# Four order edits in one fused training kernel: last forward norms, a scale and a memset, a gradient row, and the even inverse sums

## The chip, the cores and the metric

The kernel runs on one core of one Trainium2 chip. The metric is the device time of one execution in microseconds; lower is better. Before the change three runs took 1480.12, 1479.07 and 1468.7 us, so the median is 1479.07 us.

Five engines work side by side, each through its own queue in order: TensorE (PE, matmuls; its weight loads are PEld), VectorE (DVE), ScalarE (ACT), GpSimd (POOL) and SyncE (SP, which here only issues DMAs). An instruction that waits holds everything behind it in its queue.

## The reference

The kernel computes the output of one block and its nine gradients (a forward and a backward pass). Cut to what matters:

```python
def A(x, w_r, w_i):                 # spectral filter
    X = rfft2(x.astype(float32)) * (w_r + 1j * w_i)
    return irfft2(X).astype(bfloat16)
def B(x, w1, b1, w2, b2):           # channel MLP on a second layernorm
    h = gelu(layernorm(x) @ w1 + b1)
    return h @ w2 + b2
sa, ca, ga, sb, cb, gb = (silu(c) @ w_mod).reshape(6, D)
h = layernorm(x) * (1 + ca) + sa;  x = x + ga * A(h)
h = layernorm(x) * (1 + cb) + sb;  x = x + gb * B(h)
# returned: x and the gradients of x, w_r, w_i, w1, b1, w2, b2, c, w_mod
```

There are S = 2048 tokens, D = 1024 features and F = 3584 hidden features; everything is bfloat16.

## The kernel before

The order of the instructions in each queue is made when the program is built: a planner goes through the instructions with estimated times and gives each engine, whenever it is free, the ready instruction that stands first in the program (those in `tc.high_priority()` go first of all). `tc.issue_after(x)` adds, for the instructions in its block that run on x's engine, an edge of order only: they are planned behind x. `tc.add_manual_dep` does the same for one pair. Buffers of the same `tag` share one place in memory: a new tile waits until every user of the old one is done, stores included.

The tokens are four chunks of 512 (index i or b). The stages, in the order of the program:

- **Start.** Rows of `silu(c) @ w_mod` (`mod_block`), cosine and sine matrices made by POOL, DVE and ACT (`gen_mats`; `em1` holds them twice, as made and scaled), and `gBoT`, the output gradient transposed and scaled.
- **`ph_part`** (line 743): the product of `B_w2` with `gBoT`, 28 pieces. It depends on no forward work, so it fills PE between the steps of the forward spectral core.
- **First layernorm and folds.** For each chunk `ln_dve` or `ln_mix`, `norm_act`, then additions that fold tokens and features into even and odd halves (`fold_tok`, `fold_d`, `fold_pair`) into `fbuf`. `css` (tag `px0`) is cleared by a memset before the core.
- **Forward spectral core** (`spectral_core(True, ...)`): `s_fwd` for the four classes CE, SE, CO, SO (even and odd cosine and sine), eight `pair` steps, which multiply by the filter on DVE and write `R`; `s_inv` for the classes; then for each chunk `consume_fwd`. The four even-class rows of `R` are written by pairs 0 to 3, the odd ones by pairs 4 to 7.
- **`consume_fwd`** ends, for each chunk, with two layernorms: the second statistics pass is `ln_dve(tmp, 2, i)` (its square root is line 466, in `ln_fin`), then `norm_act(tmp, tmp, 2, i)` (line 500), then SP stores `tmp` to `d_n3`. `tmp` lies in `ct`, tag `fr`.
- **MLP forward**: a list written out by hand mixes `z_block` (n = 0 to 27; n = 7b + g) with steps of `bo_pass` (line 912). A `z_block` runs 32 matmuls `pz` into four PSUM banks, four ACT copies with bias into `zb` (line 864), then the gelu and its derivative on ACT (lines 866, 870, 872) and DVE (lines 867, 873 and `tt`, line 186). `hh`, the gelu, goes to one of eleven slots: `hhB` for n = 0, 1, `hhC` for 2, `hhA` for 3 to 10. `hhA` has tag `fr`. `zb` and its companions are one of two sets:

```python
n = b * 7 + g
zb, av, bv, sg, ph = gts[n % 2]
hh = hh_slots[n % 11]
```

- **MLP backward** (`pg_pass`, line 1009), with layernorm gradients, and the folds of the gradient into `fbuf2` (`fold_quarter`; the last one is `fold2_in[3]`).
- **Gradient of `w_mod`**: row r of six is made in eight steps of 128 rows. `gmod_ring` (lines 1045 to 1059) uses three buffers: SP loads a slice of `w_mod`, DVE multiplies and sums it (line 1056) and writes the product into the same buffer (line 1058), POOL stores it (line 1059). Row 5 runs before the backward core, rows 3 and 4 one step at a time beside it (`beside_bwd`), rows 2, 1, 0 after it.
- **Backward spectral core** (`spectral_core(False, ...)`). Between its steps `fill(k)` runs k products of the gradient of `w2` (line 1134; 16 matmuls each). Each pair of products needs a transposed load of `d_hh` (line 1290, `hhsA`, `hht` or part of `otl`), in a ring of three slots during the pairs; the two slots `hhsA` share tag `px1` with `au`. Four products follow each pair. `mid()` puts the last column sums between the even and the odd `s_fwd`. Before pair 6 stand the two even `s_inv`, after pair 7 the two odd ones.
- **End**: `consume_bwd` for each chunk, filled with products of the gradient of `w1` (line 1328), and the last rows of the gradient of `w_mod`.

Of the kernel before, what the change touches and what calls it, by code (L numbers as in the profile page):

```python
# [13 lines left out]
ACT = mybir.ActivationFunctionType  # L14
# [4 lines left out]
S = 2048  # L19
# [16 lines left out]
def kernel(  # L36
# [403 lines left out]
    def gen_mats():  # L440
        for cl, colv, modn in ((CE, kev, 2048), (SE, kev, 2048), (CO, kod, 4096), (SO, kod, 4096)):
            sm = (smA, smB)[cl % 2]
            rows, n = (rowo, 4) if cl % 2 else (rowe, 2)
            if cl == SE:
                nc.gpsimd.memset(kev[:, 0:1], 512.0)
            for r in range(0, n, 2):
                trig(sm[:, cl // 2, r:r + 2, :], colv, rows[r:r + 2], 2, 512, modn, cl < 2)
            nc.gpsimd.dma_start(out=d_SF[:, cl, 0:n], in_=sm[:, cl // 2])
        for cl, colv, modn in ((CE, jf[:, 0:256], 1024), (SE, jf[:, 1:257], 1024), (CO, jod, 2048), (SO, jod, 2048)):
            trig(em1[:, 0, 2 * cl:2 * cl + 2, :], colv, rowe, 2, 256, modn, cl < 2)  # L450
        nc.gpsimd.tensor_scalar(out=em1[:, 1], in0=em1[:, 0], scalar1=2.0 / (S * D), scalar2=None, op0=ALU.mult)
# [11 lines left out]
        ln_fin(sv[:, :, 2:3], sv[:, :, 1:2], sv[:, :, 3:4], 1.0 / D, row, i)  # L463

    def ln_fin(var, nmean, std, scale, row, i):
        nc.scalar.activation(out=std, in_=var, func=ACT.Sqrt, bias=eps_c[:], scale=scale)
# [28 lines left out]
        ln_fin(mv[:, :, 1:2], mv[:, :, 2:3], mv[:, :, 3:4], 1.0, row, i)  # L495

    def norm_act(out4, in4, row, i):
        for q in range(4):
            t = 4 * i + q
            nc.scalar.activation(out=out4[:, q, :], in_=in4[:, q, :], func=ACT.Identity,  # L500
                                 scale=stats[:, row, 0, t:t + 1], bias=stats[:, row, 1, t:t + 1])

    last_pu = [None]
    last_po = [None]
# [18 lines left out]
    def spectral_core(fwd, fb, sms, em, css, pt, evac_u, evac_c, evac_v, consume, o4tag, pfs=None, fill=lambda n: None, mid=lambda: None, beside=lambda n: None):  # L523
# [79 lines left out]
        def s_inv(cl, smi):  # L603
            Vt = reg.tile([P, 8, 512], BF16, name=f"V{cl}", tag=f"uv{cl}")
            Vs[cl] = Vt
            for c8 in range(8):
                dc, h = c8 // 2, c8 % 2
                k0 = (0, 1, 2, 1)[dc] + 256 * h
                base = k0 + (PW if (dc >= 2) == (cl < 2) else 0)
                pv = (ps_f if cl % 2 == 0 and c8 % 2 and not fwd else ps_s)("pv")  # L610
                for m in range(4):
                    k = (m // 2 + cl // 2) % 2
                    out, m0, m1 = (pv[:], 0, 3) if cl % 2 else (pv[:, k * 256:(k + 1) * 256], m // 2 * 2, m // 2 * 2 + 1)
                    nc.tensor.matmul(out, lhsT=R[:, cl * 4 + m, :, :].rearrange("p x w -> p (x w)")[:, base:base + 255:2],
                                     rhs=smi[:, cl // 2, m, :], start=(m == m0), stop=(m == m1))
                with tc.high_priority():
                    evac_v(Vt[:, c8, :], pv[:])
# [21 lines left out]
        pair_load(0)  # L639
        for par in range(2):  # L640
            for m in range(4):
                if par == 1 and m == 2:
                    s_inv(CE, smis[0])
                    s_inv(SE, smis[0])
                pair(par * 4 + m, par, m)
                if par * 4 + m < 7:
                    pair_load(par * 4 + m + 1)
                beside(par * 4 + m)
                if par == 0 and m == 0:
                    load_smi()  # L650
                if par == 0 and m > 0:
                    v = 0 if fwd else 1
                    if m == 1:
                        gm = reg.tile([P, 12, 256], BF16, name="gm", tag="gm")
                        for cl in (CO, SO):
                            with tc.issue_after(ld_in[0].ins):
                                nc.sync.dma_start(out=gm[:, 2 * cl:2 * cl + 2, :], in_=d_E[:, v, 2 * cl:2 * cl + 2, :])
                    else:
                        cl = (CE, SE)[m - 2]
                        for h in range(2):  # L660
                            with tc.issue_after(ld_in[0].ins):
                                nc.sync.dma_start_transpose(out=gm[:, 2 * cl:2 * cl + 2, h * P:(h + 1) * P],
                                                            in_=d_E[:, v, 2 * cl + h, :])
        s_inv(CO, smis[1])
        s_inv(SO, smis[1])
        with tc.issue_after(r_in[0].ins):
# [97 lines left out]
    for i in range(4):  # L764
        x4, fb = x4s[i], fbuf[:, i]
        if i == 0:
            with tc.issue_after(u_in.ins):
                ln_dve(x4, 0, i)
        elif i > 0:
            ln_mix(x4, 0, i, fb)  # L770
        else:
            ln_act(x4, 0, i, fb)
        norm_act(fb, x4, 0, i)
        tt(fb, fb, bcn(opca_row, 4), ALU.mult)
        fold_tok(fb, x4)
        if i % 2 == 0:
            fold_d(fb, fb, x4[:])
        else:
            pv_ = fbuf[:, i - 1]
            fold_pair(fb, pv_, fb, x4[:], x4s[i - 1][:, 0:2, :])  # L780
            tt(pv_[:, 0, :], pv_[:, 0, :], saf, ALU.add)
    css = reg.tile([P, 2, 2, 2 * PW], BF16, name="cs01", tag="px0")
    nc.gpsimd.memset(css[:], 0.0)

    def consume_fwd(i, o4, tmp, tmp2, x4, eb):
        unfold_d(o4, tmp)
# [60 lines left out]
    def z_block(b, g0, g1):  # L847
# [3 lines left out]
        for g in range(g0, g1):  # L851
# [4 lines left out]
            for k in range(4):  # L856
                fc = g * 4 + k
                pz = (ps_s, ps_d)[k % 2]("pz")
                for cch in range(NDC):
                    with ordered():  # L860
                        last_pe[0] = nc.tensor.matmul(pz[:], lhsT=w1s[g][:, cch, k * P:(k + 1) * P], rhs=n3T[:, cch, :],  # L861
                                                      start=(cch == 0), stop=(cch == NDC - 1))
                with tc.high_priority():
                    nc.scalar.activation(out=zb[:, k, :], in_=pz[:], func=ACT.Identity, bias=b1_col[:, fc:fc + 1], scale=1.0)  # L864
            with after_ev():
                nc.scalar.activation(out=av, in_=zb, func=ACT.Square)  # L866
            nc.vector.tensor_scalar(out=av, in0=av, scalar1=GC, scalar2=1.0, op0=ALU.mult, op1=ALU.add)
# [561 lines left out]
```

## Time and profile before

| | |
|---|---|
| median of three runs | 1479.07 us (1468.7 to 1480.12) |
| profiled execution, its own time | 1477.05 us |
| its span, first to last instruction | 1475.1 us |
| mean granted TensorE clock | 0.98 |
| PE busy | 1378.1 us, 93% |
| DVE busy | 1075.7 us, 73% |
| ACT busy | 749.3 us, 51% |
| POOL busy | 368.9 us, 25% |
| moved by DMA | 321.66 MB, mean 218 GB/s |

Times in the trace count from the start of the span. A row of the timeline gives the start, the duration, the engine, the line, the operation, output and input, the number of merged instructions and, in brackets, how long the engine stood idle before it and what ended that. A row of the windows gives for each engine the busy time in a stretch, then the granted clock and the share of time that the DMA engines were busy. Overlapping instructions of one engine are both counted in full, so a duration can hold a wait for a port or for a predecessor.

### The profile page before, as it was taken

To read this page: it belongs to the slowest core of one execution; us is meant where nothing else is said; L and a number is where in the kernel's file an instruction comes from. 1 tells how busy PE (TensorE), PEld (TensorE's weight loads), DVE (VectorE), ACT (ScalarE), POOL (GpSimd) and SP (SyncE) were. 2 spreads that over 40 slices of the span, in tenths; PEclk is the share of its full clock that TensorE was granted. 3 is DMA by queue.
4 is the path that set the end of the run, shared out by engine and by line. 5 is a ranking of instruction groups with operands and counts; after the bars stand their busy time and mean duration, and the time that the engine had idled before them with its cause. 6 is when DMAs were issued, how large, how long until landed. Compare 5 with 4: busy or idle time off the path is not lost. (4 is left out here: it accounts for less than half of the span.)

```text
span 1475.1 us, 18310 instructions
## 1 busy us (share of the span) xinstructions
PE 1378.1 (93%) x6705; PEld 651.9 (44%) x6835; DVE 1075.7 (73%) x1501; ACT 749.3 (51%) x1065; POOL 368.9 (25%) x446
## 2 busy tenths in 40 slices
PE   4979999899599999999999999999998989999997
PEld 2535555444244444444444444444554535444443
DVE  5995878797799787887520899887566677998633
ACT  4675555768787765666206563332522425443211
POOL 5620631201012122112111011010334431322423
PEclk9999999999899999999999999999999999999999
DMA  9962564799488867698998266287699998667994
GB/s 334 280 214 72 152 206 149 243 299 324 172 219 270 262 233 253 195 277 224 266 281 242 96 233 228 84 233 169 178 216 226 249 216 213 189 191 196 241 235 164
DMA packets 356063, 321.66 MB, mean 218 GB/s; under 512 B 207210, under 2 KB 298880, under 8 KB 355846
## 3 DMA queue, kind: packets, MB, share of 16 engines
q1 hardware_dynamic: 321990, 206.14, 52.8%
q0 software_dynamic: 33984, 114.36, 22.6%
q8 instruction: 53, 0.87, 0.3%
q14 instruction: 36, 0.29, 0.1%
HBM read 161.01 MB, written 110.15 MB: 184 GB/s over the span
## 5 line engine op out<-in xcount | busy, mean ns | idle before, releaser
L743 PE MATMUL pp<-gBoT,wt 128*128 128x512 bf16 x872 | 197.3, 382 | 7.1 <-DVE pho L749 5.8
L1009 PE MATMUL pg<-w1T,gzr 128*128 128x512 bf16 x877 | 196.9, 383 | 1.0
L1328 PE MATMUL gw1acc<-gzh,n3n 128*128 128x512 bf16 x876 | 193.8, 379 | 3.4 <-DMA gzh<-d_gz 2.4
L861 PEld LDWEIGHTS <-w 128*128 128x128 bf16 x896 | 87.5, 98 | 123.4 <-issue 20.0
L743 PEld LDWEIGHTS <-wt 128*128 128x128 bf16 x896 | 87.6, 98 | 110.5 <-issue 8.7
L1009 PEld LDWEIGHTS <-gzr 128*128 128x128 bf16 x896 | 87.3, 98 | 109.4 <-issue 7.2
L1328 PEld LDWEIGHTS <-n3n 128*128 128x128 bf16 x896 | 87.2, 98 | 107.8 <-issue 3.8
L861 PE MATMUL pz<-n3Ta,w 128*128 128x512 bf16 x440 | 99.5, 384 | 16.0 <-ACT gt L864 15.7
L1134 PE MATMUL gw2acc<-gB,hhsA 128*128 128x512 bf16 x438 | 99.4, 384 | 4.6 <-DMA hhsA<-d_hh 4.0
L861 PE MATMUL pz<-n3Tb,w 128*128 128x512 bf16 x437 | 98.4, 379 | 0.7 <-ACT gt L864 0.2
L912 PEld LDWEIGHTS <-hhA 128*128 128x128 bf16 x608 | 59.4, 98 | 75.0 <-issue 5.5
L864 ACT ACTIVATE gt<-pz,b_col 128x512 bf16<-128x512 f32 x112 | 72.7, 683 | 36.2 <-PE pz L861 35.7
L1141 ACT CAST gwo<-gw2acc 128x512 bf16<-128x512 f32 x46 | 26.7, 583 | 120.8 <-PE gw2acc L1134 75.8
L1332 ACT CAST gwo<-gw1acc 128x512 bf16<-128x512 f32 x50 | 29.1, 583 | 112.2 <-PE gw1acc L1328 92.1
L186 DVE TENSOR_TENSOR gt<-gt,gt 128x2048 bf16<-128x2048 bf16 x56 | 68.4, 1224 | 21.8 <-ACT gt L872 20.6
L186 DVE TENSOR_TENSOR ct<-ct 128x2048 bf16<-128x2048 bf16 x68 | 80.5, 1220 | 0.6
L870 ACT ACTIVATE gt<-gt 128x2048 bf16<-128x2048 bf16 x28 | 53.5, 1911 | 53.7 <-DVE gt L186 53.7
L1056 DVE CUSTOM_DVE_ANT_0 otl<-otl 128x1024 bf16<-128x1024 bf16 x24 | 29.1, 1224 | 55.9 <-DMA otl<-in_w_mod_dram 44.8
L1134 PEld LDWEIGHTS <-hhsA 128*128 128x128 bf16 x448 | 43.9, 99 | 57.7 <-DMA hhsA<-d_hh 5.1
L749 ACT CAST pho<-pp 128x512 bf16<-128x512 f32 x62 | 35.8, 582 | 45.9 <-PE pp L743 45.2
L866 ACT ACTIVATE gt<-gt 128x2048 bf16<-128x2048 bf16 x28 | 53.4, 1908 | 4.8 <-DVE w2sA L186 2.3
L872 ACT ACTIVATE gt<-gt 128x2048 bf16<-128x2048 bf16 x28 | 53.5, 1909 | 0.5
(335 smaller groups left out, 2535.3 us busy)
## 6 DMA issues: line engine op xcount, KB each, us to landing
gzr<-d_gz SPq DMA_DIRECT2D x28, 512.0 KB
wblk<-in_w_mod_dram SPq DMA_DIRECT2D x12, 1024.0 KB
out_dram<-otl POOLq DMA_DIRECT2D x48, 256.0 KB, 3.4
out_dram<-gwo POOLq DMA_DIRECT2D x96, 128.0 KB, 4.1
d_ph<-pho POOLq DMA_DIRECT2D x21, 512.0 KB, 4.4
d_hh<-hhA POOLq DMA_DIRECT2D x19, 512.0 KB, 5.0
w2sD<-in_B_w_dram SPq DMA_DIRECT2D x14, 512.0 KB
w2sA<-d_ph SPq DMA_DIRECT2D x14, 512.0 KB
```

The source lines that it names most:

```text
L186: return nc.vector.tensor_tensor(out=out, in0=a, in1=b, op=op)
L743: last_pe[0] = nc.tensor.matmul(pp[:], lhsT=wt[:, fg % 2, cch, k * P:(k + 1) * P], rhs=gBoT[j][:, cch, :], start=(cch == 0), stop=(cch == ...
L749: nc.any.tensor_copy(out=ov, in_=pv)
L861: last_pe[0] = nc.tensor.matmul(pz[:], lhsT=w1s[g][:, cch, k * P:(k + 1) * P], rhs=n3T[:, cch, :], start=(cch == 0), stop=(cch == NDC - 1))
L864: nc.scalar.activation(out=zb[:, k, :], in_=pz[:], func=ACT.Identity, bias=b1_col[:, fc:fc + 1], scale=1.0)
L866: nc.scalar.activation(out=av, in_=zb, func=ACT.Square)
L870: nc.scalar.activation(out=sg, in_=bv, func=ACT.Sigmoid, scale=2.0 * GK)
L872: nc.scalar.activation(out=bv, in_=bv, func=ACT.Sigmoid, scale=-2.0 * GK)
L912: last_pe[0] = nc.tensor.matmul(pbs[i][:], lhsT=hh[:, k, i * P:(i + 1) * P], rhs=wp[:, k, :], start=False, stop=(g == 6 and k == 3))
L1009: last_pg[0] = nc.tensor.matmul(pgs[i][:], lhsT=gzs[b, g][:, k, i * P:(i + 1) * P], rhs=w1Ts[g][:, k, h * KH:(h + 1) * KH], start=(g == 0 ...
L1134: nc.tensor.matmul(acc[:], lhsT=hh_of(fc)[:, t, :], rhs=gBs[t // 4][:, t % 4, h * KH:(h + 1) * KH], start=(t == 0), stop=(t == NT - 1))
L1328: nc.tensor.matmul(acc[:], lhsT=n3ns[t // 4][:, t % 4, cch * P:(cch + 1) * P], rhs=gz2[t // 8][:, t % 8, :], start=(t == 0), stop=(t == NT ...
```

## The change

Four edits, independent of each other:

1. In `gen_mats` the scaled copy of `em1` moves from POOL to ACT. The memset of `css` moves from POOL to DVE and is ordered behind the last addition of the forward fold.
2. The square root of the last chunk's last forward layernorm is ordered behind the fourth PSUM copy of `z_block` n = 3, and its four `norm_act` instructions behind the fourth PSUM copy of n = 4.
3. In the backward core the two even `s_inv` move from ahead of pair 6 to behind pair 7 and its fills. The forward core keeps them ahead of pair 6.
4. The DVE instructions of row 5 of the gradient of `w_mod` are ordered behind the last gradient fold.

```diff
-        nc.gpsimd.tensor_scalar(out=em1[:, 1], in0=em1[:, 0], scalar1=2.0 / (S * D), scalar2=None, op0=ALU.mult)
+        nc.scalar.mul(out=em1[:, 1], in_=em1[:, 0], mul=2.0 / (S * D))
...
-        nc.scalar.activation(out=std, in_=var, func=ACT.Sqrt, bias=eps_c[:], scale=scale)
+        sqrt_in[0] = nc.scalar.activation(out=std, in_=var, func=ACT.Sqrt, bias=eps_c[:], scale=scale)
...
     def norm_act(out4, in4, row, i):
+        norm_in[0] = ()
         for q in range(4):
             t = 4 * i + q
-            nc.scalar.activation(out=out4[:, q, :], ...)
+            norm_in[0] += (nc.scalar.activation(out=out4[:, q, :], ...),)
+
+    sqrt_in, norm_in = [None], [()]
+
+    def behind(ins, later):
+        tc.add_manual_dep(ins.ins, later.ins.name, mybir.DependencyInfo(mybir.DependencyClass.NoSync, mybir.DependencyReason.DATA),
+                          reason="order")
...
-                if par == 1 and m == 2:
+                if fwd and par == 1 and m == 2:
                     s_inv(CE, smis[0])
                     s_inv(SE, smis[0])
                 pair(par * 4 + m, par, m)
...
+        if not fwd:
+            s_inv(CE, smis[0])
+            s_inv(SE, smis[0])
         s_inv(CO, smis[1])
         s_inv(SO, smis[1])
...
-            tt(pv_[:, 0, :], pv_[:, 0, :], saf, ALU.add)
+            fold_in = tt(pv_[:, 0, :], pv_[:, 0, :], saf, ALU.add)
     css = reg.tile([P, 2, 2, 2 * PW], BF16, name="cs01", tag="px0")
-    nc.gpsimd.memset(css[:], 0.0)
+    with tc.issue_after(fold_in.ins):
+        nc.vector.memset(css[:], 0.0)
...
+    n3_sqrt, n3_norm = sqrt_in[0], norm_in[0]
...
-                    nc.scalar.activation(out=zb[:, k, :], in_=pz[:], func=ACT.Identity, bias=b1_col[:, fc:fc + 1], scale=1.0)
+                    z_in = nc.scalar.activation(out=zb[:, k, :], in_=pz[:], func=ACT.Identity, bias=b1_col[:, fc:fc + 1], scale=1.0)
+            if n == 3:
+                behind(n3_sqrt, z_in)
+            elif n == 4:
+                for ins in n3_norm:
+                    behind(ins, z_in)
...
-    for _ in gmod_ring((5,), gmy, sacc):
-        pass
+    with tc.issue_after(fold2_in[NB - 1].ins):
+        for _ in gmod_ring((5,), gmy, sacc):
+            pass
```

More of the change, by code (lines that the diff above doesn't have):

```diff
@@ L497, in norm_act @@
     def norm_act(out4, in4, row, i):
+        norm_in[0] = ()
         for q in range(4):
             t = 4 * i + q
-            nc.scalar.activation(out=out4[:, q, :], in_=in4[:, q, :], func=ACT.Identity,
-                                 scale=stats[:, row, 0, t:t + 1], bias=stats[:, row, 1, t:t + 1])
+            norm_in[0] += (nc.scalar.activation(out=out4[:, q, :], in_=in4[:, q, :], func=ACT.Identity,
+                                                scale=stats[:, row, 0, t:t + 1], bias=stats[:, row, 1, t:t + 1]),)
+    sqrt_in, norm_in = [None], [()]
+    def behind(ins, later):
+        tc.add_manual_dep(ins.ins, later.ins.name, mybir.DependencyInfo(mybir.DependencyClass.NoSync, mybir.DependencyReason.DATA),
+                          reason="order")
     last_pu = [None]
```

## The prediction

> **What bounds the kernel now.** I read the page first, then windows of 25 us for all engines, then PE's timeline around each window in which PE stands idle, and last the timelines of DVE, ACT, POOL and SP around the stalls that the change touches.
>
> The page says PE is the engine to follow. The windows (busy time of PE, PEld, DVE, ACT, POOL, then granted clock, DMA share and GB/s) say where it isn't full:
>
> ```profile
> span 1475.1 us, 18310 instructions
> PE 1378.1 (93%) x6705; PEld 651.9 (44%) x6835; DVE 1075.7 (73%) x1501; ACT 749.3 (51%) x1065; POOL 368.9 (25%) x446
> ...
> 375.00:400.00 25.00, 12.64 (x51) 5.38 (x51) 17.41 (x27) 16.11 (x15) 1.54 (x2) 0.80 0.42 147
> ...
> 450.00:475.00 25.00, 24.89 (x120) 10.94 (x121) 24.47 (x24) 19.21 (x18) 5.93 (x7) 1.00 0.76 250
> ...
> 1025.00:1050.00 25.00, 18.88 (x116) 11.26 (x117) 15.94 (x24) 12.84 (x24) 8.72 (x11) 0.93 0.55 166
> ...
> 1150.00:1175.00 25.00, 22.17 (x132) 13.25 (x133) 15.99 (x23) 12.64 (x24) 10.56 (x11) 0.93 0.97 260
> ```
>
> PE's own timeline names what ended each of these idle times (in brackets):
>
> ```profile
> 59.68 13.76 PE L743 MATMUL pp<-gBoT,wt 128*128 128x512 bf16 x62
> ...
> 79.22 3.57 PE L743 MATMUL pp<-gBoT,wt 128*128 128x512 bf16 x8 [5.78 <-DVE pho L749]
> ...
> 390.11 8.64 PE L861 MATMUL pz<-n3Ta,w 128*128 128x512 bf16 x31 [12.31 <-ACT gt L864]
> 405.60 6.85 PE L861 MATMUL pz<-n3Ta,w 128*128 128x512 bf16 x31 [3.40 <-ACT gt L864]
> 415.96 7.07 PE L861 MATMUL pz<-n3Ta,w 128*128 128x512 bf16 x32
> ...
> 1035.72 8.36 PE L517 MATMUL pu<-smA,fbuf 128*128 128x256 bf16 x63 [5.87 <-DVE fbuf L186]
> ...
> 1154.11 8.77 PE L1134 MATMUL gw2acc<-gB,otl 128*128 128x512 bf16 x31 [2.73 <-DMA otl<-d_hh]
> 1162.72 7.58 PE L614 MATMUL pv<-smi,R 128*128 128x256 bf16 x64
> ...
> 1201.26 0.81 PE L614 MATMUL pv<-smB,R 128*128 128x512 bf16 x3
> 1207.21 1.46 PE L614 MATMUL pv<-smB,R 128*128 128x512 bf16 x3 [5.14 <-DVE R L186]
> ```
>
> Each of the four edits touches one of these idle times. The reader should also see that a long idle time costs more than itself: the eight matmuls after 5.78 us take 3.57 us, at the usual 13.76/62 = 0.222 us they would take 1.78. The windows with the holes are those with a clock under 1.00.
>
> **Edit 1, the scale and the memset.** Timelines of POOL, DVE and ACT at 69 to 78 us:
>
> ```profile
> 68.70 5.40 POOL L451 TENSOR_SCALAR em<-em 128x2048 bf16<-128x2048 bf16 x1
> 69.00 5.14 DVE L491 TENSOR_SCALAR mv<-mv 128x2 f32<-128x2 f32 x1
> 74.16 3.52 POOL L783 MEMSET cs<- 128x4112 bf16 x1
> 74.19 3.52 DVE L488 TENSOR_SCALAR mv<-mv 128x2 f32<-128x2 f32 x1
> 74.23 1.15 ACT L493 ACTIVATE fbuf<-x,mv 128x1024 bf16<-128x1024 bf16 x1 [4.32 <-DVE mv L487]
> 78.01 4.63 ACT L500 ACTIVATE fbuf<-x,stats 128x1024 bf16<-128x1024 bf16 x4 [2.54 <-DVE stats L186]
> ```
>
> A DVE instruction on two numbers per lane lasts 5.14 us and ends within 0.05 us of POOL's scale; the next lasts 3.52 us and ends with POOL's memset. DVE is shut out while POOL works, and PE's copy `pho` waits behind. Both POOL instructions go. PE gets 5.78 back and the slow matmuls' 3.57 - 1.78 = 1.79, together 7.57 us; DVE, whose fold feeds PE later, gets most of 5.14 + 3.52 = 8.66 back, so it does not become the new wait. I expect the forward stages up to 375 us to keep the gain: PE is full there or waits for DVE chains that move with it.
>
> What is added: an ACT pass over 128x2048. The gelu's passes of that shape take 1.91 us (53.4/28, below); it falls into ACT's idle 4.32 or 2.54 us above and costs nothing, or 1.9 if it lands elsewhere. And a DVE memset of 4112 elements behind the last addition of the fold. DVE's pass over 4096 elements takes 2.29 us, POOL's memset 3.52; queued behind it are DVE's share of the `U` copies, for which PE's two banks wait. I take 1.0 us on the path, between 0 (ACT copies meanwhile) and 3.5. Against the move speaks the Trainium skill, "VectorE: DVE Perf Modes", section "Zero memsets can be issued as uint32 (trn2)": a memset takes one cycle per element whatever the type, unless a zero memset is issued as uint32, with half the elements. At the 0.96 GHz that the skill gives for this engine ("Trainium Kernel Development and Optimization", section "NeuronCore Architecture") that is an estimate of 4.3 or 2.1 us; by the first, all of it on the path, the sum would be 3.3 us worse. No row here shows a DVE memset of this size.
>
> ```profile
> L866 ACT ACTIVATE gt<-gt 128x2048 bf16<-128x2048 bf16 x28 | 53.4, 1908 | 4.8 <-DVE w2sA L186 2.3 <-DVE hhC L186 1.9
> 370.35 2.29 DVE L186 TENSOR_TENSOR ct<-ct,rows 128x4096 bf16<-128x4096 bf16 x1 [6.44 <-ACT ct L500]
> ```
>
> Edit 1: -7.57 + 1.0 = **-6.6 us** (bounds -7.6 and -2.2).
>
> **Edit 2, the last norms.** The largest hole, 12.31 us, is put down to the copies of n = 3 (line 864). What did these wait for? ACT and DVE from 374 us:
>
> ```profile
> 382.23 0.64 DVE L867 TENSOR_SCALAR gt<-gt 128x2048 bf16<-128x2048 bf16 x1
> 382.35 0.30 ACT L466 ACTIVATE mv<-mv,eps_c 128x4 f32<-128x4 f32 x1 [5.14 <-DVE mv L477]
> 382.67 1.28 ACT L870 ACT_TABLE_LOAD   x1
> 385.31 1.91 ACT L870 ACTIVATE gt<-gt 128x2048 bf16<-128x2048 bf16 x1 [1.36 <-DVE gt L186]
> 387.13 2.36 ACT L500 ACTIVATE ct<-ct,stats 128x1024 bf16<-128x1024 bf16 x2
> 387.25 1.22 DVE L186 TENSOR_TENSOR hhB<-gt,gt 128x2048 bf16<-128x2048 bf16 x1 [0.16 <-ACT gt L870]
> 389.39 2.39 ACT L864 ACTIVATE gt<-pz,b_col 128x512 bf16<-128x512 f32 x4
> ...
> 404.88 2.40 ACT L864 ACTIVATE gt<-pz,b_col 128x512 bf16<-128x512 f32 x4
> 411.52 1.22 DVE L186 TENSOR_TENSOR hhA<-gt,gt 128x2048 bf16<-128x2048 bf16 x1
> ...
> DMA to landing us min/median/max: 9.5/9.5/9.5
> ```
>
> The copies of n = 3 write `zb` of set 1, whose last reader is `hh` of n = 1 (`hhB`), done at 387.25 + 1.22 = 388.47. The two norms before the copies cost 389.39 - 388.47 = 0.9 us, no more. `hh` waits for the sigmoid of n = 1, that for DVE, and DVE came to line 867 only at 382.23 because the statistics of the same layernorm stood before it; these don't move. The copies of n = 4 wait in the same way for `hh` of n = 2. So the 12.31 us stay, but for 0.3 to 0.9. Later, where two norms went (2.36 us), ACT gets the square root with two table loads of 1.28 (2 x 1.28 + 0.3 = 2.9 us): nothing is won. Queued behind: the four norms now follow the copies of n = 4 (4 x 1.2 = 4.7 us), then SP's store of `d_n3`, and `hh` of n = 3 is the first write to `hhA`, which has the place of `ct` and must wait until the store has landed. Say that the copies of n = 4 come 4 us earlier (401), so that PE's wait of 3.40 goes: then the norms run from 403 to 408, and with a landing 9.5 us later, as the store of the chunk before took (last row), or in half of that, `hhA` is written at 413 to 417 instead of 411.52, holding DVE and then the copies of n = 5 and PE at 415.96. PE has gained 0.9 + 3.4 by then and may lose 3. I take **0 us** (bounds -17.5, the whole 12.31 + 1.8 of slow matmuls + 3.40, and +14, a store that SP issues only when PE is as far as now at 415.96: 415.96 + 9.5 - 411.52). A gain here would also meet DVE, 24.47 of 25 us busy at 450.
>
> **Edit 4, row 5.** DVE at the last gradient fold, and the release of `au`:
>
> ```profile
> 1023.27 1.23 DVE L1056 CUSTOM_DVE_ANT_0 otl<-otl 128x1024 bf16<-128x1024 bf16 x1 [4.95 <-issue]
> ...
> 1054.62 0.67 DVE L186 TENSOR_TENSOR rows<-acc3b,au 64x512 bf16<-64x512 f32 x1
> 1055.32 5.05 SPq L1290 DMA_TRANSPOSE hhsA<-d_hh  x2
> ```
>
> The first step of row 5 stands in the middle of the fold and waits 4.95 us for its load; the multiply-and-sum of the second step, 1.23 too, also lies before the fold's end. Behind the fold they free 4.95 + 2 x 1.23 = 7.4 us of DVE, so the fold ends near 1035.7 - 7.4 = 1028.3 and PE, free at 1035.72 - 5.87 = 1029.85, does not wait: -5.87, and 8.36 - 7.58 = 0.8 for slow matmuls. Against it: the eight steps now begin at 1028, and behind them in DVE's queue may stand the `rows` copy that frees `au`, on which the transposed loads for the next products hang (SP, 1055.32). The ring took 1054.6 - 1023.3 = 31.3 us; the same from 1028.3 would end at 1059.6, 5 us later than now, and with 1.8 us of slow matmuls (edit 1) cost 6.8. But its first slices, one for each of the three buffers, are loaded by then, so that three steps follow at once; I expect its end near where it is now, the copies before it, and PE's next product a little late. Value **-5.5 us** (bounds -6.7 and +6.8).
>
> **Edit 3, the even sums.** PE waits 5.14 us for pair 7's `R`. DVE is late there because it waited for a load of row 4 ahead of pair 6:
>
> ```profile
> 1183.06 1.23 DVE L1056 CUSTOM_DVE_ANT_0 otl<-otl 128x1024 bf16<-128x1024 bf16 x1 [7.39 <-DMA otl<-in_w_mod_dram]
> 1184.73 1.29 DVE L186 TENSOR_TENSOR Pt<-cs01b 128x1028 bf16<-128x1028 bf16 x2
> 1206.45 1.30 DVE L186 TENSOR_TENSOR R<-qa 128x1026 bf16<-128x1026 bf16 x2
> ```
>
> Without the even sums (1162.72, 7.58 us) ahead of it, pair 6 is 7.6 us earlier on PE, and the step at 1183 should fall behind it. The three steps beside pair 6 still cost most of their wait, so that `R` gains less than the 7.6: about 1203 by my estimate, between 1207.7 (now) and 1200. PE has the same work in another order and gets there at 1201.3 or a little later. The odd sums effectively start at 1203.5 instead of 1207.21 - 0.81 = 1206.4: -2.9, and -0.8 for the slow matmuls (three in 1.46 us for 0.67). Against it: the even sums need no DMA, and they stood where PE waits for DMA (2.73 us at 1154.11, share 0.97). Value **-3.7 us** (bounds -5.9 and +7.6, all that cover lost again).
>
> **The sum**: -6.6 + 0 - 5.5 - 3.7 = -15.8, from the profiled execution's 1477.05 us (span 1475.1 and 1.95 around it): **1461 us**. That execution is 2.0 us under the median of 1479.07.
>
> **Rivals.**
>
> (a) The forecast, 1461 us, own range 1453 to 1468: 45%.
>
> (b) Only edit 1 pays. The pair steps are paced by SP's loads, not by PE or DVE (DMA share 0.97), and what edits 3 and 4 give is waited for at the next load: 1477 - 6.6 = 1470 us. For it: PE's 2.73 us wait for `otl`. Against: DMA share 0.55 at 1025, where edit 4 acts. 20%.
>
> (c) Edit 2 costs: `hhA` is held by the late store, +9 to +14 before z block 6, not made good since DVE is full to 475: 1461 + 10 = 1471 us. For it the 9.5 us landing, against it the quiet DMA there (0.42). 15%.
>
> (d) Edit 2 does what its name says and the profile's attribution is right: the hole at 390 closes by most of 15.7 + 1.8; with DVE full at 450 some 15 remain: 1446 us. Against it: `hhB` at 388.47. 13%.
>
> (e) Slower: the SP queue sets the backward core. Row 5 ends late, the loads behind `au` come 5 us late (+6.8), and pairs 6 and 7 lose their cover and wait for transposed loads (+7.6, and 2 x 1.7 for two slow restarts such as 8.77 instead of 7.07 us): 17.8 - 6.6 = +11.2, 1488 us. For it: the 2.73 us at 1154.11. Against: such a wait is not in every pair. It decides once the loads of line 1290 land later than PE wants them in each pair. 7%.
>
> **Numbers.** The range 1448 to 1478 holds (a), (b) and (c) and leaves (d) and (e), 20%. A measurement of this kernel can tell about 1% from no change, 14.8 us: faster means under 1464.3. Of (a) 80% lies there, all of (d), little else: 0.51. Slower by over 1%, over 1493.9, is only the far end of (e) and what I don't see: 0.07. The rest, 0.42.
>
> **What would show it.** Right: no DVE row of microseconds on 128x2 at 69 to 78 and PE idle under 1 us there; a hole of about 11 us still before z block 4; PE going into the even `s_fwd` near 1029.9 - 6.6 = 1023 without waiting for `fbuf`; the even sums behind the last fills, and less than 2.5 us before the odd ones. Wrong: that hole gone, a new hole before z block 6, waits for `hhsA` or `otl` grown by over 5 us in total, or a DVE memset over 3.5 us with PE idle at the first `s_fwd`.

## The result, and the profile after

The changed kernel takes 1485.25 us in the median of 22 runs (1480.87 to 1495.35), the kernel before 1479.14 us (22 runs, 1468.7 to 1488.48). The ratio is 1.0054, 95% interval 1.0035 to 1.0073: 0.54% slower, some 8 us by the means of the runs (the medians stand 6.1 us apart), above the range of the prediction. The profiled execution took 1490.29 us. Its page, and the windows that were read before, with one more:

```profile
span 1487.8 us, 18437 instructions
PE 1391.0 (93%) x6835; PEld 654.5 (44%) x6835; DVE 1071.6 (72%) x1503; ACT 751.1 (50%) x1065; POOL 355.2 (24%) x444
...
375.00:400.00 25.00, 13.44 (x56) 5.70 (x55) 20.25 (x30) 16.93 (x17) 2.28 (x3) 0.80 0.29 102
...
1025.00:1050.00 25.00, 23.47 (x146) 13.44 (x145) 10.21 (x21) 18.92 (x35) 8.91 (x12) 1.00 0.62 200
1150.00:1175.00 25.00, 22.30 (x106) 10.31 (x105) 14.79 (x22) 5.96 (x10) 8.58 (x10) 0.94 1.09 241
1200.00:1225.00 25.00, 12.27 (x72) 7.95 (x72) 7.82 (x12) 11.63 (x22) 6.79 (x9) 0.73 1.08 209
```

The window at 1025 is nearly full now and that at 375 is as empty as before. At 1200 PE works for 12.27 us, where the kernel before has 19.59:

```profile
1200.00:1225.00 25.00, 19.59 (x88) 9.21 (x89) 12.07 (x18) 10.51 (x19) 7.28 (x9) 0.86 1.09 244
```

PE's timeline of the changed kernel names the holes (line numbers have moved up by 7 to 17):

```profile
121.44 0.83 PE L524 MATMUL pu<-smA,fbuf 128*128 128x256 bf16 x6 [1.26 <-DVE fbuf L186]
...
321.06 9.36 PE L753 MATMUL pp<-gBoT,wt 128*128 128x512 bf16 x32 [4.77 <-DMA wt<-in_B_w_dram]
...
387.31 8.66 PE L873 MATMUL pz<-n3Ta,w 128*128 128x512 bf16 x32 [11.56 <-ACT gt L876]
414.87 8.54 PE L873 MATMUL pz<-n3Ta,w 128*128 128x512 bf16 x32 [5.09 <-ACT gt L876]
...
1026.10 7.31 PE L524 MATMUL pu<-smA,fbuf 128*128 128x256 bf16 x64
...
1052.27 2.29 PE L558 MATMUL pcs<-empf,U 128*128 128x256 bf16 x12 [3.54 <-DVE rows L186]
1057.84 16.51 PE L1151 MATMUL gw2acc<-gB,hhsA 128*128 128x512 bf16 x64 [3.28 <-DMA hhsA<-d_hh]
...
1196.80 1.91 PE L621 MATMUL pv<-smi,R 128*128 128x256 bf16 x16
1212.73 7.27 PE L621 MATMUL pv<-smi,R 128*128 128x256 bf16 x48 [14.02 <-ACT V L719]
1219.84 13.98 PE L621 MATMUL pv<-smB,R 128*128 128x512 bf16 x64
1233.65 5.40 PE L693 MATMUL po<-gm,V 128*128 128x256 bf16 x48
```

Three of the four idle times that the edits aimed at are gone: the 5.78 us at `pho` (at 69 to 78 us no DVE row on 128x2 is longer than 0.27 us), the 5.87 at `fbuf` (1026.10 starts without waiting) and the 5.14 before the odd sums. None of it reaches the end. PE came to the first `po` of the backward core at 1222.99 and comes now at 1233.65. The largest new hole is that of 14.02 us in the even sums, which edit 3 put there.

### The profile page after: what moved, and what is told of

It reads as the page before. It is cut to its first block, busy times and chain, and to the rows that moved or that the text cites. A ratio compares the mean times of both kernels' runs of the same rounds, so it can differ in the third digit from the quotient of the medians.

```text
span 1487.8 us, 18437 instructions
## 1 busy us (share of the span) xinstructions
PE 1391.0 (93%) x6835; PEld 654.5 (44%) x6835; DVE 1071.6 (72%) x1503; ACT 751.1 (50%) x1065; POOL 355.2 (24%) x444
## 5 line engine op out<-in xcount | busy, mean ns | idle before, releaser
L753 PE MATMUL pp<-gBoT,wt 128*128 128x512 bf16 x896 | 200.4, 382 | 4.8 <-DMA wt<-in_B_w_dram 4.8
L1151 PE MATMUL gw2acc<-gB,hhsA 128*128 128x512 bf16 x448 | 105.8, 398 | 11.4 <-DMA hhsA<-d_hh 8.7
L1158 ACT CAST gwo<-gw2acc 128x512 bf16<-128x512 f32 x46 | 26.7, 583 | 138.2 <-PE gw2acc L1151 85.0
```

Source lines behind the costliest of these rows:

```text
L753: last_pe[0] = nc.tensor.matmul(pp[:], lhsT=wt[:, fg % 2, cch, k * P:(k + 1) * P], rhs=gBoT[j][:, cch, :], start=(cch == 0), stop=(cch == ...
L1151: nc.tensor.matmul(acc[:], lhsT=hh_of(fc)[:, t, :], rhs=gBs[t // 4][:, t % 4, h * KH:(h + 1) * KH], start=(t == 0), stop=(t == NT - 1))
```

## The experiments

Each kernel ran on one chip beside the kernel before; ratios are to that. For all kernels PE's timeline also gives three stretches that depend little on how early a stage is reached: from the first matmul of z block 0 to that of z block 7; from the first even `s_fwd` matmul of the backward core to the first product of its pairs ("ring"); from there to the first `po` ("pairs"). In the kernel before they are 426.65 - 332.31 = 94.3, 1060.51 - 1029.58 = 30.9 and 1222.99 - 1060.51 = 162.5 us:

```profile
332.31 7.07 PE L861 MATMUL pz<-n3Ta,w 128*128 128x512 bf16 x32
...
426.65 7.07 PE L861 MATMUL pz<-n3Tb,w 128*128 128x512 bf16 x32 [0.17 <-ACT gt L864]
...
1029.58 0.27 PE L517 MATMUL pu<-smA,fbuf 128*128 128x256 bf16 x1
...
1060.51 13.99 PE L1134 MATMUL gw2acc<-gB,hhsA 128*128 128x512 bf16 x63
...
1222.99 5.40 PE L683 MATMUL po<-gm,V 128*128 128x256 bf16 x48
```

| edits | ratio (95%) | z 0 to 7 | ring | pairs |
|---|---|---|---|---|
| none | 1 | 94.3 | 30.9 | 162.5 |
| 1 | 0.9974 (0.9953 to 0.9995) | 95.5 | 26.0 | 167.4 |
| 2 | 1.0011 (0.9988 to 1.0034) | 97.6 | 31.5 | 164.6 |
| 3 | 1.0040 (1.0016 to 1.0064) | 94.4 | 31.3 | 173.4 |
| 4 | 1.0018 (0.9996 to 1.0040) | 95.9 | 32.4 | 165.8 |
| 1, 2 | 0.9993 (0.9969 to 1.0016) | 98.8 | 26.7 | 166.0 |
| 1, 4 | 0.9973 (0.9946 to 1.0000) | 95.5 | 31.4 | 164.3 |
| 2, 4 | 1.0039 (1.0015 to 1.0063) | 98.6 | 31.7 | 162.4 |
| 1, 2, 4 | 1.0036 (1.0017 to 1.0054) | 98.7 | 30.8 | 169.9 |
| 1, 2, 3, 4 | 1.0054 (1.0035 to 1.0073) | 96.4 | 31.7 | 175.8 |
| 4, `au` freed first | 0.9988 (0.9968 to 1.0008) | 95.8 | 23.8 | 166.6 |
| 1, 4, `au` freed first | 0.9962 (0.9941 to 0.9983) | 95.5 | 23.8 | 166.6 |
| none, two rows unstored | 1.0014 (0.9992 to 1.0036) | 94.5 | 31.8 | 163.7 |
| 3, two rows unstored | 0.9989 (0.9963 to 1.0014) | 94.5 | 32.0 | 156.3 |
| 3, even `V` on DVE | 1.0045 (1.0020 to 1.0069) | 95.5 | 31.2 | see below |
| 3, stores by ACT | 1.0058 (1.0034 to 1.0082) | 95.5 | 31.2 | 176.0 |
| 1, 3, 4, `au` first, stores by ACT | 0.9997 (0.9973 to 1.0020) | 95.5 | 23.8 | 177.7 |
| all, both waits gone | 0.9949 (0.9924 to 0.9975) | 98.7 | 23.8 | 160.4 |

**One edit at a time.**

```diff
+ nc.scalar.mul(out=em1[:, 1], ...)  ;  css: nc.vector.memset behind the fold      # edit 1
+ behind(n3_sqrt, z_in)  at n == 3   ;  behind(ins, z_in) for the norms at n == 4   # edit 2
+ if not fwd: s_inv(CE, ...); s_inv(SE, ...)  behind the pair loop                  # edit 3
+ with tc.issue_after(fold2_in[NB - 1].ins):  around gmod_ring((5,), gmy, sacc)     # edit 4
```

> Edit 1 alone. Theory (from the two traces): the start gains about 5 us up to the first even s_fwd, but the last ph_part products before the MLP wait for the transposed load of wt (4.77 us in the changed kernel's trace), so only 2 to 5 us are left at the end: 1474 to 1477 us against 1479, and that wait for wt at about 321 us shows here too, as no other edit acts before it. Rival (the prediction's term): the gain is kept, -6.6 us, 1472.5, and the wait for wt belongs to another cause and is under 1 us here.

1472.84 us beside 1477.54, -0.26%: a gain. The interval reaches to 6.9 us and so holds the 6.6 predicted; the mean over five kernels below does not. The wait for `wt` is there (5.48 us), and in all eight profiles with edit 1 (4.55 to 6.34 us); without it no profile has more than 0.58. The first matmul of z block 0 comes at 329.7 us on average of these eight and at 330.8 of the ten others. So little of the 5 us that `s_fwd` behind the fold gained is left there. Coming early does not by itself bring the wait: two profiles without edit 1 (those without the hole at `pho`, see the last section) reach z block 0 at 327.4 and 327.7 us, earlier than any with edit 1, and wait at most 0.31 us for `wt`. Why the load is late with edit 1 stays open. More of the gain lies where nobody looked for it, in the ring, 26.0 and 26.7 us in the two profiles with edit 1 and without edit 4 against 30.9 to 32.0 in seven without both. There DVE stands idle for 2.0 and 2.5 us ahead of the first step of row 5, instead of 4.2 to 5.0; the rows name no releaser ("issue"), and why it is less was not tried. Nor is the ring the whole of the gain: beside edit 4 it is as long with edit 1 as without, and edit 1 gains there too, by the mean below.

> Edit 2 alone. Theory: worth nothing, -2 to +2 us; the hole before z block 4 stays above 10 us, the 3.4 us wait before z block 5 goes, and a new one of about 5 us stands before z block 6. Rival (c) of the prediction: it costs, since the write of hhA waits for the late store of d_n3 and what is gained before is given back with more, +5 to +10 us. Second rival: it is a real gain of 4 us or more that the changed kernel loses elsewhere.

1479.65 us, a ratio that tells nothing alone. The stretch does: 96.4 to 98.8 us in the six profiles with edit 2, 94.3 to 95.9 in the twelve without, 2.9 us more on average. The holes are those of the theory: 11.91 us before z block 4, none before 5, 5.18 before 6. DVE's timeline of this kernel has rival (c):

```profile
415.83 1.23 DVE L186 TENSOR_TENSOR hhA<-gt,gt 128x2048 bf16<-128x2048 bf16 x1 [2.08 <-DMA d_n<-ct]
```

`hhA` waits until the late store of `d_n3` has landed. The rest of the hole before z block 6 is ACT's own: four norms of 1.2 us stand between the copies of n = 4 and the gelu passes.

> Edit 3 alone: the even s_inv of the backward core behind pair 7 and its fills. Theory: this is where the change loses, +7 to +12 us (1486 to 1491), because PE's wait ahead of the odd sums is held not by DVE's R alone but by ACT, whose copies of V stand in its queue behind a copy of gwo that waits for a store of gwo to land; the even sums (7.6 us of PE) lose their cover and that wait stays: a hole of more than 8 us before the rest of the even sums, ended by ACT's V. Rival (the prediction's term): -3.7 us, and a wait under 2.5 us before the odd sums. Second rival: 0, PE's work is only in another order.

1483.9 us, +0.40%: a loss, as this theory had it. ACT, PE and POOL of this kernel:

```profile
1206.63 0.59 ACT L1144 CAST gwo<-gw2acc 128x512 bf16<-128x512 f32 x1 [14.80 <-DMA out_dram<-gwo]
1207.11 3.13 ACT L712 CAST V<-pv 128x512 bf16<-128x512 f32 x6
...
1207.75 7.03 PE L614 MATMUL pv<-smi,R 128*128 128x256 bf16 x48 [14.36 <-ACT V L712]
...
1194.98 0.58 POOL L1146 DMA_DIRECT2D out_dram<-gwo  x1
```

The copies of `V` follow, in ACT's queue, a copy of `gwo` that waits 14.80 us for a store of the same half row, four products earlier. PE fills its free PSUM banks with 16 matmuls of the even sums and stops.

> Edit 4 alone. Theory: the even s_fwd of the backward core starts some 6 to 10 us earlier, but row 5's steps then end behind the au release no earlier than before, the transposed loads of hhsA come at the same time and PE waits there: -1 to +1 us by pair 1 and at the end. Rival (the prediction's term): -5.5 us are kept. Second rival: the later ring costs, +3 to +7 us.

1479.71 us, no gain. PE goes into the even `s_fwd` without a wait, yet the ring is as long as before (32.4 us). In the changed kernel DVE and SP show why:

```profile
1021.67 2.48 DVE L186 TENSOR_TENSOR fbuf<-fbuf,gzr 128x2048 bf16<-128x2048 bf16 x2
...
1038.72 1.23 DVE L1073 CUSTOM_DVE_ANT_0 otl<-otl 128x1024 bf16<-128x1024 bf16 x1 [9.82 <-DMA otl<-in_w_mod_dram]
...
1048.45 1.23 DVE L1073 CUSTOM_DVE_ANT_0 otl<-otl 128x1024 bf16<-128x1024 bf16 x1 [4.90 <-DMA otl<-in_w_mod_dram]
...
1051.54 0.68 DVE L186 TENSOR_TENSOR rows<-acc3b,au 64x512 bf16<-64x512 f32 x1
...
1052.24 4.85 SPq L1307 DMA_TRANSPOSE hhsA<-d_hh  x2
```

The fold ends at 1024.15, three steps run on buffers already loaded, and the others wait for their loads. The addition that frees `au` stands behind all eight, and the transposed loads behind that.

**What edit 3's wait hangs on.**

```diff
+ if fc in (20, 21): return        # ahead of the store in gw2_out, on edit 3 and on the kernel before
+ (evac_v if fwd or cl % 2 else dve_copy)(Vt[:, c8, :], pv[:])                # even V on DVE
+ (nc.scalar if fc < 24 else nc.gpsimd).dma_start(out=out_6[...], in_=row[:, half])   # stores by ACT
```

> Edit 3 alone, and the stores of rows fc = 20 and 21 of the gradient of w2 are left out (four stores of 128 KB, 1 MB of output less two halves: those rows of the output are not written). The copies of fc = 22 and 23, which overwrite the same two rows of gwo, then wait for no store. Theory: the 14.4 us hole before the rest of the even sums goes (under 3 us left), as ACT's copies of V no longer stand behind a waiting copy of gwo: 9 to 12 us faster than edit 3 alone (1483.9), so 1472 to 1475, 3 to 6 below before. Rival: the hole is R or DVE or DMA bandwidth; it moves to another releaser and less than 4 us come back, 1480 or more.

> The kernel before with the same stores of rows fc = 20 and 21 left out (those rows are not written), the control for the run before. Theory: in the kernel before PE's wait ahead of the odd sums (5.14 us) was put down to DVE's R at 1207.2, and the ACT copy of gwo ended at 1207.9, so both held it; with the store wait gone R still holds it: 0 to -2 us. Rival: the store was the whole wait, -5 us.

1471.9 and 1476.75 us beside 1475.25. The first ratio is 0.51% under that of edit 3 alone, 7.5 us with an interval of about 5, where 9 to 12 were expected. PE and ACT of edit 3 without those stores:

```profile
1186.62 7.31 PE L614 MATMUL pv<-smi,R 128*128 128x256 bf16 x64
1193.88 14.21 PE L614 MATMUL pv<-smB,R 128*128 128x512 bf16 x64
1207.92 5.40 PE L686 MATMUL po<-gm,V 128*128 128x256 bf16 x48
...
1186.87 0.59 ACT L1144 CAST gwo<-gw2acc 128x512 bf16<-128x512 f32 x1 [2.87 <-PE gw2acc L1137]
```

From the even sums to `po` nothing waits any more, and the pairs take 156.3 instead of 173.4 us. In the control PE still waits 5.10 us for `R`: there the store was hidden beside `R`. The two ratios differ by 0.0025, 3.7 us with an interval of about 5 to both sides: what edit 3 would be worth without that wait, against a cost of 5.9 us with it.

> Edit 3 alone, with the PSUM copies of the two even s_inv of the backward core on DVE instead of ACT. Theory: the copies no longer stand behind ACT's copy of gwo, so the hole before the rest of the even sums is cut from 14.4 us to what DVE's queue leaves (R of pair 7 and the steps of row 4 until about 10 us after the fills), some 4 to 8 us faster than edit 3 alone: 1476 to 1480. The odd sums' copies on ACT still stand behind the gwo copy. Rival: R is what is late; no change against edit 3 alone, 1484.

1480.13 us, 1.0045 (1.0020 to 1.0069): no better than edit 3 alone at the end, though the hole shrinks as foreseen. Two lines of PE:

```profile
1204.86 2.72 PE L614 MATMUL pv<-smi,R 128*128 128x256 bf16 x12 [9.70 <-DVE V L715]
1208.13 3.65 PE L614 MATMUL pv<-smi,R 128*128 128x256 bf16 x32 [0.55 <-ACT gwo L1144]
```

DVE gets to `V` only behind pair 7's work, and the odd sums start at 1214.87, where edit 3 alone has 1214.62. But both profiles begin their pairs at 1055.1, and this one comes to the even sums 1.8 us later (1193.25 against 1191.48) and does 3.3 us of later work, `po` among it, ahead of the odd sums, so that its stretch up to the first `po` doesn't compare. So some 5 us are won at this place. The two ratios, 0.05% apart with an interval of about 0.34, can't tell whether they reach the end.

> Edit 3 alone, and the stores of gwo for fc = 8 to 23 are issued by ACT's queue right behind each copy, not by POOL's. Everything is stored. Theory: in edit 3 alone the last store that ACT's copy waits for is issued late, because POOL's queue is held by the stores of pf, empf and row 4, which wait for DVE; from ACT's queue it goes out at once, lands some 6 us later (the median of these stores), and the 14.4 us hole shrinks below 4: 6 to 10 us faster than edit 3 alone (+5.9), so -4 to 0 us against before. Rival: it is the landing that is slow (11 us at the busiest time of the DMA engines), not POOL's queue; then the hole keeps 8 us or more, and the time is within 3 us of edit 3 alone.

1488.62 us beside 1481.53: no help, but not for the reason of the rival. The wait moved into ACT's own DMA issue:

```profile
1211.89 0.34 ACTq L1146 DMA_DIRECT2D out_dram<-gwo  x1
1212.27 1.07 ACT L712 CAST V<-pv 128x512 bf16<-128x512 f32 x2 [13.83 <-DMA n3n<-d_n]
```

The issue of the last store holds ACT for 13.8 us. The trace puts the end of that down to loads of `n3n`, which the store has no need of. In the same stretch SP's issue of a transposed load takes 12.36 us (1202.29 to 1214.65); what held the two is not shown. The run therefore doesn't part POOL's queue from the landing. The changed kernel's own rows give a share to both:

```profile
1182.57 0.59 ACT L1158 CAST gwo<-gw2acc 128x512 bf16<-128x512 f32 x1 [4.17 <-PE pcs L558]
...
1211.61 0.59 ACT L1158 CAST gwo<-gw2acc 128x512 bf16<-128x512 f32 x1 [14.53 <-DMA out_dram<-gwo]
...
1192.36 0.54 POOL L1076 DMA_DIRECT2D out_dram<-otl  x1 [10.12 <-DVE otl L1075]
...
1200.27 0.58 POOL L1160 DMA_DIRECT2D out_dram<-gwo  x1
```

Counted back from the last, the copy at 1182.57 is the one that the store at 1200.27 takes away, and the copy at 1211.61 overwrites the same half row. So the data lay ready for 17 us while POOL stood behind stores that wait for DVE, and by the end of ACT's wait the store took 11 more to land. More rows for `gwo`, or another order of POOL's stores, would part the two; neither was tried.

**What edit 4's ring hangs on.**

```diff
+ halves_in[0] = tt(row, acc[0:64, :], odd, ALU.add)            # frees au
+ for ins in ring_in[3:8]: behind(ins, halves_in[0])            # steps 3 to 7 of row 5
```

> Edit 4 alone, with steps 3 to 7 of row 5 ordered on DVE behind the addition that frees au (rows<-acc3b,au). Theory: the 9.6 us that edit 4 gains at the even s_fwd were lost because that addition stands behind all eight steps, whose loads of w_mod come late; ahead of them it frees au about 15 us earlier, the transposed loads of hhsA follow, and PE's waits of 4.3 (rows) and 2.8 us (hhsA) before the first products of the pair stage go: 5 to 9 us faster at pair 1 than with edit 4 alone. At the end 1472 to 1476 if that is kept. Rival (b) of the prediction: the pairs are paced by SP's loads, what is gained at pair 1 is waited for at later loads of hhsA and otl, and the end is within 2 us of edit 4 alone (1479.7).

1471.74 us beside 1475.25. PE and DVE:

```profile
1049.05 13.98 PE L1140 MATMUL gw2acc<-gB,hhsA 128*128 128x512 bf16 x64
...
1108.93 8.70 PE L1140 MATMUL gw2acc<-gB,hhsA 128*128 128x512 bf16 x32 [5.09 <-DMA hhsA<-d_hh]
...
1034.59 0.68 DVE L186 TENSOR_TENSOR rows<-acc3b,au 64x512 bf16<-64x512 f32 x1 [5.84 <-ACT au L226]
```

The addition runs at 1034.59, the ring takes 23.8 us in all four profiles with this order, and the products start without a wait. That is 7.6 us less than the usual 31.4. The pairs then take 166.6 us, where the nine kernels with the usual order and without edit 3 take 165.2 on average (162.4 to 169.9): rival (b) is there in the waits of 5.09 and 3.52 us for loads, but takes back little at this place. At the end edit 4 is 0.30% faster with this order than without it, 4.4 us, with an interval as large; beside edit 1 the same two orders differ by 0.11%. The gain in the ring is plain, how much of it reaches the end is not.

**The edits together.**

> Edits 1, 2 and 4, the changed kernel with the even sums of the backward core back ahead of pair 6. Theory: edit 3 is the whole slowdown; the single runs add up to -3.8 + 1.6 + 2.6 = +0.4 us, so 0 to +2 us against before, within what can be told from no change, and 5 to 8 us under the changed kernel. Rival: the edits hinder each other (edit 1's gain is eaten by the wait for wt and the hole before z block 6), and this is 4 us or more slower than before.

1485.94 us beside 1481.53, +0.36%. That theory fell: edit 3 is not the whole slowdown. In this profile PE waits 9.00 us for `R` ahead of the odd sums, where the kernel before waits 5.14; why was not followed up. In the kernels that follow the other three are taken in pairs, with nothing else changed.

> Edits 1 and 2. Theory A (no hindrance): the single runs add, -3.8 + 1.6 = -2.2 us, ratio 0.9985 or 0.3% at most about it. Theory B (edit 2 eats edit 1's forward gain: the late d_n3 store and the norms on ACT make the hole before z block 6 whatever time PE arrives): no faster than edit 2 alone, ratio 1.001 to 1.004.

> Edits 1 and 4, au not freed first. Theory A: -3.8 + 2.6 = -1.2 us, ratio 0.999. Theory B (edit 1 brings the kernel earlier to the backward core, where edit 4's ring holds au all the same, so edit 1's gain is lost there): ratio 1.001 to 1.003. In either case PE's stretch from the first even s_fwd matmul to the first product of the pair stage is 31 to 32 us, as in the kernel before and in edit 4 alone, and not the 24 us of the runs with au freed first.

> Edits 2 and 4. Theory A: +1.6 + 2.6 = +4.2 us, ratio 1.003. Theory C (edits 2 and 4 make the loss of 0.36% and edit 1 adds nothing when they are there): 1.0035 to 1.006.

1476.11, 1473.72 and 1482.51 us beside 1476.01. Edits 1 and 2 (0.9993) and edits 1 and 4 (0.9973) lie by theory A; B lies outside the interval of the second and at the edge of that of the first. For edits 2 and 4 (1.0039) the interval holds both A and C. Take for each edit the kernels that differ in it alone, and the mean of their differences: edit 1 -0.24% (five), edit 2 +0.29% (four), edit 4 +0.22% (four), edit 3 +0.29% (two). A single difference has an interval of 0.2 to 0.35% to both sides, a mean of some 0.15 to 0.2. The four add up to +0.56%; measured were 0.54. That sum can't show whether two edits hinder each other, since in such means what each pair does to the other cancels. The eight kernels with and without edits 1, 2 and 4 (`au` not freed first) can: edit 2 costs 0.16% without edit 1 and 0.41 with it, 0.15% without edit 4 and 0.42 with it, both differences within an interval of about 0.3, so a hindrance is neither shown nor excluded; between edits 1 and 4 none is seen (0.02). What misled was adding three single runs, whose sum is only known to 0.4%. One thing does depend on company: edit 1's 5 us in the ring are gone once edit 4 is there (31.4 us for 1 and 4).

> Edits 1 and 4, with au freed ahead of steps 3 to 7 of row 5: the version that the single runs point to. Theory: edit 1 gives 3.8 us and edit 4 with au first 1.8 to 3.5 (its ratio 0.9988; 1471.7 against 1475.25), other stages, so they add: -5 to -8 us, 1469 to 1472 beside 1477, faster than both kernels. Rival: what edit 1 brings to the backward core is waited for at the same loads of hhsA and otl, and only one of the two gains is left, -2 to -4 us.

1474.81 us beside 1481.53, -0.38%: the lowest ratio of the kernels that do all the work, and faster than the kernels before and after the change. Edit 1 alone and edits 1 and 4 (0.9974 and 0.9973) lie within its interval.

> Edits 1, 3 and 4 with au freed first and the stores of gwo for fc = 8 to 23 issued by ACT. Theory: with the store wait out of ACT's queue edit 3 gives what the prediction said of it (the runs with the two rows unstored stood 0.25% apart, 3.7 us), so 2 to 4 us below edits 1 and 4 with au first. Rival: ACT's DMA issues or the late landings keep a hole of 4 us or more before the even sums, and this is level with edits 1 and 4 with au first or slower.

1480.46 us beside 1481.53, 0.9997 (0.9973 to 1.0020). With the stores issued by ACT a wait of 11.98 us for `V` stays in front of the odd sums, so edit 3 takes back what the others gave. The rival was right.

> All four edits, with au freed ahead of steps 3 to 7 of row 5, and the stores of rows fc = 20 and 21 of the gradient of w2 left out (those rows are not written), so that ACT's copies of V stand behind no waiting copy of gwo. Theory: the two waits are the loss; without them the changed kernel loses what edit 3's run lost by the store (0.5%) and edit 4's by the au release (0.3%): 1.0054 - 0.008 = 0.997 of before, about 1474 to 1476 beside 1480. Rival: something else in the combination costs, and it stays at 1.001 or above.

1470.26 us beside 1476.01, -0.51%, more than the 0.3 expected. With the two waits away the change that lost 0.54% wins about as much, though edit 2 still costs its 3 us (98.7). The missing stores by themselves showed no gain in the control (1.0014, at best 0.9992).

## Why the prediction was wrong

**Edit 3, -3.7 predicted, +4.3 measured (0.29%).** The failed step is "PE has the same work in another order and gets there at 1201.3 or a little later", and with it "the odd sums effectively start at 1203.5": in the changed kernel they start at 1219.84, behind the hole of 14.02 us. The prediction read the 5.14 us before them as DVE's `R` alone, as the releaser said, and looked for what makes `R` earlier. Two engines held that place. Lines of ACT in the kernel before, which the prediction did not look up:

```profile
1207.38 0.58 ACT L1141 CAST gwo<-gw2acc 128x512 bf16<-128x512 f32 x1 [8.74 <-DMA out_dram<-gwo]
1207.86 0.59 ACT L709 CAST V<-pv 128x512 bf16<-128x512 f32 x1
```

ACT was free for `V` only 0.65 us after PE's wait ended. In the changed kernel DVE has written `R` by 1204.7, but the moved even sums need ACT first, and ACT waits until 1211.61:

```profile
1203.38 1.30 DVE L186 TENSOR_TENSOR R<-qa 128x1026 bf16<-128x1026 bf16 x2
```

What the term described is worth 3.7 us by the two runs without the stores. That it is the very number predicted is luck, as the interval is about 5 us and the pairs of the two differ by 7.4. The bound above, +7.6 for lost cover, held the loss; the cause given with it, late transposed loads, was the wrong one: PE's waits for `hhsA` and `otl` in the pairs come to 6.7 us in the kernel before and to 7.7 with edit 3 alone.

**Edit 4, -5.5 predicted, +3.3 measured (0.22%).** PE reaches the even `s_fwd` and goes on, as said, and three steps follow at once, as said. The failed step is "I expect its end near where it is now, the copies before it": the addition that frees `au` came behind all eight steps and not before them. The bound +6.8 had this order, with too long a ring: from the first step to that addition it is 27.4 us with edit 4 alone (1023.32 to 1050.75), not the 31.3 carried over. The value was taken from the other end without a look at which of the two the planner would put first. That order decides whether the ring gives anything (23.8 instead of 32.4 us); the ratios go the same way, -0.12% instead of +0.18%, at the edge of what their intervals can tell. The 4.95 us that the prediction called a wait for a load have no releaser in their row ("issue"); behind the fold they are gone, as forecast. With the usual order the ring is about as long with edit 4 as without it (1.5 and 0.2 us more in the two comparisons without edit 1), so nothing is won there; beside edit 1, whose short ring is lost, it is 5.4 and 4.1 us longer. Why the ratio is higher without edit 1 too is not shown.

**Edit 1, -6.6 predicted, -3.5 measured (0.24%).** The hole and the long DVE rows went. PE came to its first matmul of `s_fwd` 110.42 - 103.18 = 7.2 us earlier, but DVE's fold let it go on only 126.29 - 121.44 = 4.9 us earlier. The later matmuls in the kernel before:

```profile
126.29 0.83 PE L517 MATMUL pu<-smA,fbuf 128*128 128x256 bf16 x6 [0.60 <-DVE fbuf L186]
```

So DVE's share, "gets most of 5.14 + 3.52 = 8.66 back", was put too high. The step that failed for most of the rest is "I expect the forward stages up to 375 us to keep the gain": a transposed load of `wt` is waited for. The 1.0 us set for the memset was not spent, since PE waits for nothing behind it up to 132 us. A view of the tile `css` in the changed kernel:

```profile
L794 DVE MEMSET cs<- x1: 1772/1772/1772, 121.8 to 121.8; 128x2056 uint32 x1
```

The Trainium skill, "VectorE: DVE Perf Modes", section "Zero memsets can be issued as uint32 (trn2)", told of half the elements in this form. The row agrees, 2056 for 4112; at 1.77 us it is shorter than the estimate of 2.1 that was worked out from the Trainium skill's clock.

**Edit 2, 0 predicted, +4.2 measured (0.29%).** Each row came out as argued: the hole of 12.31 us stays (11.56), as it was held by the gelu before it; the 3.40 us go; `hhA` waits for the store of `d_n3`. The failed step is the balance, "PE has gained 0.9 + 3.4 by then and may lose 3": from z block 0 to 7 it loses 2.9 us net, so some 7 against about 4 gained. The norms' 4.7 us on ACT had been counted only on the way to the store, not as a delay of the gelu behind them.

**The whole.** Rival (c) had the right mechanism for edit 2, at over twice its size, and (e) the right order for row 5 and the right sign, at 7%. That the 1488 us of (e) lie near the measured 1485.25 is luck: its cause for edit 3 is not the one found, its +6.8 and +11.0 are two to three times what was measured, and it has nothing for edit 2. Of the signs set down for right, no long DVE row, a hole of 11.56 us before z block 4, no wait for `fbuf` and none before the odd sums came true; of those for wrong, the new hole before z block 6 (5.09 us). The hole of 14.02 us stood in neither list. The range failed because the costs of edits 2, 3 and 4 were each put at or near their good ends and their bad ends treated as separate chances, with none for all three at once. Edits 3 and 4 share a fault of reading: a stage full of waits was priced by the wait that ended last, and the next one was not looked up. For edit 2 it was work put on ACT ahead of the gelu that had no price.

## What to carry to other kernels

A releaser in the profile is the one that ended last; before work is moved to that place, read every queue that the moved work needs there, here ACT's copies and the POOL stores behind them, and ask when each would have been free. Here a step that was moved ahead of a ring of loads shortened the stage only once what frees the next loads was moved ahead as well. And single-edit runs must be as precise as the question: differences of 0.3% come out of several kernels that differ in one edit, and out of the length of a stretch in the trace, not out of one ratio.

## What the runs showed of the hardware

The 5.78 us hole at `pho` depends on which of two instructions starts first. It is there in eight of the ten profiles without edit 1 (4.89 to 5.80 us) and not in the other two, whose instructions at this place are the same. In the kernel with edit 3 and two rows unstored, DVE and then POOL:

```profile
67.92 0.15 DVE L491 TENSOR_SCALAR mv<-mv 128x2 f32<-128x2 f32 x1
...
69.62 2.94 DVE L186 TENSOR_TENSOR stats<-mv,stats 128x4 f32<-128x4 f32 x1
...
73.09 0.67 DVE L752 CAST pho<-pp 128x512 bf16<-128x512 f32 x1
...
68.88 5.40 POOL L451 TENSOR_SCALAR em<-em 128x2048 bf16<-128x2048 bf16 x1
```

There DVE's instruction on 128x2 starts a microsecond before POOL's scale and lasts 0.15 us; in the kernel before it starts 0.3 us after it and lasts 5.14. The Trainium skill, "SBUF — State Buffer", section "🔬 SBUF: two separate sides", says that DVE, in its two-port modes or with two inputs in SBUF, and GpSimd share one pair of ports as an exclusive lock, held for a whole instruction by whichever starts first; these two rows agree with it. The row of 2.94 us fits less well: it starts 0.7 us behind POOL's scale and ends 1.7 us ahead of the scale's end (72.56 against 74.28).

Two profiles of the same instructions can stand 10 us apart in the middle of the span: the backward core's first `s_fwd` matmul starts at 1029.58 in the kernel before and at 1019.60 in the kernel with edit 3 and two rows unstored, which has the same instructions in the same order on every engine up to there. The ring right behind it takes 30.9 and 32.0 us in the two, so stretches compare where starts don't.
